# A layer-norm root begun on GpSimd, and sums and copies placed elsewhere in their queues

## The chip, the core and the metric

The kernel runs on one core of a Trainium2 chip. The metric is the device time of one execution, in microseconds. The core has TensorE (matrix products; PE, and PEld for its weight loads), VectorE (DVE), ScalarE (ACT), GpSimd (POOL) and SyncE (SP, which here issues the DMAs). Each engine works through its own queue in order; an instruction that waits holds up everything behind it on its engine.

## What is computed

Attention in blocks of 64 tokens, then two feed-forward layers over 4608 tokens of width 512. The reference, cut to what matters:

```python
scores = q_c @ k_c.T / sqrt(64); attn = softmax(scores); x = attn @ v_c      # chunks of 64
# first layer, 512 -> 2048 -> 512
h = x @ w_in;  g = h * clip(h + 3, 0, 6) / 6;  x = g @ w_out
# second layer, 512 -> 1024 -> 512
h = x @ w_in2
sm = exp(h - max(h)) / (sum(exp(h - max(h))) + 1e-9)
solu = h * sm
mu = mean(solu);  var = mean((solu - mu) ** 2)
out = ((solu - mu) / sqrt(var + 1e-6) * g_ln) @ w_out2
```

## The kernel before, in words

All products run in fp32 split into two parts (`hi`, a rounded copy made by ScalarE, and `lo`, the rest, made by a subtraction on VectorE or GpSimd), each product as three: hi by hi, hi by lo, lo by hi.

The first layer goes over 9 blocks of 512 tokens and, in each, over 16 slices `f` of the hidden width. For each slice `moe_h` makes h (L376), `moe_gate` the gate on VectorE (L386), `moe_split` the hi cast on ScalarE (L393) and the lo subtraction on VectorE (L396), and `moe_o` adds to the block's sum (L407). The attention of the next block is put between the slices.

The second layer works on pairs `p` of 128-token tiles (18 pairs, tiles 2p and 2p+1). Its first product is a two-by-two block product by Strassen's scheme: seven products `product_1` to `product_7` of six matmuls each (L560) in three PSUM banks a, b and c. `fetch_x2` (L520, SP) loads a pair's x, `combine_x2` (L525 to L528, four VectorE instructions) makes the sums and differences S1 to S4, `split_x2` makes hi on ScalarE (L534, L535) and lo on GpSimd (L541). The results are gathered while the banks go on being used: `product_1` is followed by a copy of bank a on ScalarE (L583), which `product_2` must wait for because it goes on adding to a; `sum_2` reads bank b on VectorE (L592), and `product_7` must wait for it; `sums_7` reads b and c (L611, L612), and `product_4` must wait for L611.

Then for each tile: `soft_1` (maximum L627 on VectorE, exponential with its sum L630 on ScalarE), `soft_2` (L635 to L642 on VectorE, of which L638 is the product of two SBUF operands over 128x1024), `turn` (a 32 by 32 transpose L648 on VectorE, and then copies of 32 partitions each (L666) by DMAs on SP, by ScalarE and for some tiles by GpSimd), `chain_square` (sum of squares, ScalarE, L673), `split_l` (hi on ScalarE, lo on GpSimd, L734 and L738), `out_mm` (24 matmuls, L754, called in turn by `out_next`), `out_store` (scaling by the root, ScalarE, L763, and the DMA out), called by `stores`. `chain_rstd` makes the inverse root of the variance of a pair of tiles: a shift of the bit pattern, a seed constant less that, and three Newton steps. Before, its first three instructions (L679, L684, L687, 128x2 each) are on VectorE, the twelve of the Newton steps (L692 to L697) on GpSimd.

The order on every engine is the order in which the code is written: it is a hand-made sequence. In slices 11 to 15 of the last block the products of pair 0 are mixed in; pairs 1, 2 and 3 have sequences of their own behind that, and pairs 4 to 17 run the `for p in range(3, NP)` loop. The prediction calls three stretches stage 1 (slice 15 and pair 1), stage 2 (the products of pair 3 up to `product_2(3)` and `product_7(3)`) and stage 3 (from tile 3's `out_mm` over `product_4(3)` to the products of pair 4).

Of the kernel before, what the change touches and what calls it, by code (L numbers as in the profile page):

```python
# [10 lines left out]
I32 = mybir.dt.int32  # L11
AF = mybir.ActivationFunctionType
ALU = mybir.AluOpType
# [8 lines left out]
def tile_kernel(  # L22
# [653 lines left out]

    def chain_rstd(p):
        va = va_t.pop(p)
        nc.vector.tensor_scalar(  # L679
            out=va, in0=va, scalar1=1.0 / FF2, scalar2=1e-6, op0=ALU.mult, op1=ALU.add  # L680
        )
        y = bs.tile([P, 2], F32, tag="y", name="y", bufs=4)
        yi = y.bitcast(I32)
        nc.vector.tensor_single_scalar(  # L684
            out=yi, in_=va.bitcast(I32), scalar=1, op=ALU.logical_shift_right
        )
        nc.vector.tensor_scalar(  # L687
            out=yi, in0=yi, scalar1=-1.0, scalar2=float(RSQRT_SEED), op0=ALU.mult, op1=ALU.add
        )
        tt = bs.tile([P, 2], F32, tag="tt", name="tt")  # L690
        for _ in range(3):
            nc.gpsimd.tensor_mul(out=tt, in0=y, in1=y)  # L692
            nc.gpsimd.tensor_mul(out=tt, in0=tt, in1=va)
            nc.gpsimd.tensor_scalar(
                out=tt, in0=tt, scalar1=-0.5, scalar2=1.5, op0=ALU.mult, op1=ALU.add
            )
            nc.gpsimd.tensor_mul(out=y, in0=y, in1=tt)  # L697
        for i in range(2):
            rs_t[2 * p + i] = y[:, i : i + 1]
# [147 lines left out]
    for b in range(NB):  # L847
# [3 lines left out]
        for f in range(NF):  # L851
# [9 lines left out]
            else:  # L861
                if last:
                    split_w(3 if f == 10 else 1, nc.vector)
                g = moe_split(t, nc.vector)
            pend.append((b, f, g))
            if f % 4 == 3:
                slot(b, f)
# [14 lines left out]
            if last:  # L882
# [16 lines left out]
                    fetch_x2(2)  # L899
                for step in EARLY.get(f, ()):  # L900
                    step(0)
                if f == 14:
                    combine_x2(1)
                elif f == 15:
                    combine_x2(2)
    while pend:
        moe_o(*pend.pop(0))
    put("2", NF - 1, late.pop(NF - 1))
# [5 lines left out]
    ps_2 = ctx.enter_context(tc.tile_pool(name="ps_2", bufs=2, space=PSUM, reuse_waits="tile"))  # L914

    product_1(1)
    split_x2(2)
    fetch_x2(3)
    soft_1(1)
    product_6(1)  # L920
    sum_2(1)
    soft_1(0)
    product_2(1)
    product_7(1)
# [31 lines left out]
    chain_rstd(0)  # L956
    out_next()
    soft_2(3)
    turn(3)
    fetch_x2(4)  # L960
    square(3)
    soft_1(5)
    soft_2(2)
    out_next()
    product_1(3)
    product_6(3)
    sum_2(3)
    turn(2)
# [13 lines left out]
    for p in range(3, NP):  # L982
        last = 2 * p - 2
        if p > 3:
            product_1(p)
            split_l(last - 2)
            stores()
            product_6(p)
            product_5(p)
            sum_2(p)  # L990
# [20 lines left out]
        chain_rstd(p - 1)  # L1011
        product_4(p)
        product_3(p)
        stores()
        out_next()
        soft_first(p)
    split_l(last)
# [79 lines left out]
```

## Time and profile before

| what | value |
|---|---|
| median of 3 runs | 1289.9 us (1288.97 to 1291.45) |
| the profiled execution, its own time | 1289.6 us |
| its span, first to last instruction | 1287.8 us |
| TensorE busy | 1247.7 us (97% of the span), 6260 matmuls |
| VectorE busy | 908.9 us (71%) |
| ScalarE busy | 597.4 us (46%) |
| GpSimd busy | 252.2 us (20%) |
| mean granted TensorE clock | 0.992 |

The rest, 1.8 us, lies around the span. The granted clock is given as a share of full speed: 1.00 is 2.4 GHz and 0.50 is 1.2 GHz. Read the waits of TensorE first, since it is the busiest engine, then the timelines of the other engines at the places where TensorE waits. Lines are those of the kernel before.

### The profile page before, as it was taken

To read this page: it belongs to the slowest core of one execution; us is meant where nothing else is said; L and a number is where in the kernel's file an instruction comes from. 1 tells how busy PE (TensorE), PEld (TensorE's weight loads), DVE (VectorE), ACT (ScalarE), POOL (GpSimd) and SP (SyncE) were. 2 spreads that over 40 slices of the span, in tenths; PEclk is the share of its full clock that TensorE was granted. 3 is DMA by queue.
4 is the path that set the end of the run, shared out by engine and by line. 5 is a ranking of instruction groups with operands and counts; after the bars stand their busy time and mean duration, and the time that the engine had idled before them with its cause. 6 is when DMAs were issued, how large, how long until landed. Compare 5 with 4: busy or idle time off the path is not lost.

```text
span 1287.8 us, 17624 instructions
## 1 busy us (share of the span) xinstructions
PE 1247.7 (97%) x6260; PEld 1024.5 (80%) x6260; DVE 908.9 (71%) x1720; ACT 597.4 (46%) x1097; POOL 252.2 (20%) x333
## 2 busy tenths in 40 slices
PE   5899999999999999999999999999869999999998
PEld 4688888888888888888888888887658888888887
DVE  6999556556556565565565565599888888888884
ACT  4776322222222222222322322463567777777775
POOL 1000000000000000000000000002456676666755
PEclk9999999999999999999999999999889999999999
DMA  9901101101101101101101100450112222323211
GB/s 320 374 26 47 61 25 44 64 25 48 59 25 49 58 25 50 58 25 50 58 25 50 58 25 1 147 180 17 58 50 81 90 89 77 95 70 95 91 56 64
DMA packets 68391, 93.70 MB, mean 73 GB/s; under 512 B 10192, under 2 KB 39120, under 8 KB 68304
## 3 DMA queue, kind: packets, MB, share of 16 engines
q1 hardware_dynamic: 68304, 92.58, 22.1%
q8 instruction: 49, 0.80, 0.3%
q14 instruction: 38, 0.31, 0.1%
HBM read 62.92 MB, written 18.87 MB: 64 GB/s over the span
## 4 chain that ended last, share of the span: by engine, by line
PE 86%; DVE 10%; ACT 2%; issue 1%; SPq 1%; DMA 1%; POOL 0%; DVEq 0%; ACTq 0%
PE acc L407 27%; PE hp L376 27%; PE po L754 14%; PE b L560 5%; PE c L560 4%; PE a L560 3%; PE att L355 3%; PE att L279 2%; DVE s L181 2%; DVE t L386 1%; ACT g_hi L393 1%; DVE s L173 1%; DVE g_lo L396 1%; DVE pbd L345 0%; DVE wo L181 0%
## 5 line engine op out<-in xcount | busy, mean ns | idle before, releaser
L407 PE MATMUL acc<-g_hi,wo 128*128 128x512 f32 x1152 | 289.3, 393 | 1.7 <-ACT g_hi L393 1.7
L376 PE MATMUL hp<-x_hi,wi 128*128 128x512 f32 x1152 | 285.7, 390 | 4.1 <-ACT wi L255 2.6
L382 ACT ACTIVATE t<-hp,three 128x512 f32<-128x512 f32 x144 | 99.1, 688 | 375.1 <-PE hp L376 374.6
L376 PEld LDWEIGHTS hp<-x_hi,wi 128*128 128x128 f32 x1152 | 215.6, 188 | 50.1 <-ACT wi L255 3.5
L407 PEld LDWEIGHTS acc<-g_hi,wo 128*128 128x128 f32 x1152 | 213.6, 188 | 51.3 <-issue 5.3
L386 DVE SCALAR_TENSOR_TENSOR t<-t,hp 128x512 f32<-128x512 f32 x144 | 98.9, 687 | 205.2 <-ACT t L382 205.1
L77 POOL TENSOR_TENSOR wi<-s,wi 128x512 fp32r<-128x512 f32 x5 | 7.3, 1453 | 875.4 <-ACT wi L76 869.1
L396 DVE TENSOR_TENSOR g_lo<-t,g_hi 128x512 fp32r<-128x512 f32 x144 | 99.6, 692 | 83.6 <-ACT g_hi L393 83.0
L407 PE MATMUL acc<-g_lo,wo 128*128 128x512 f32 x576 | 154.1, 389 | 0.0
L376 PE MATMUL hp<-x_lo,wi 128*128 128x512 f32 x576 | 153.9, 389 | 0.0
L754 PE MATMUL po<-wi,wo 128*128 128x512 f32 x648 | 150.8, 389 | 0.0
L393 ACT CAST g_hi<-t 128x512 fp32r<-128x512 f32 x144 | 89.3, 620 | 121.6 <-DVE t L386 121.6
L754 PEld LDWEIGHTS po<-wi,wo 128*128 128x128 f32 x648 | 121.5, 188 | 25.4 <-POOL wo L738 0.2
L345 DVE STREAM_TRANSPOSE pbd<-p 32x128 f32<-32x128 f32 x448 | 135.5, 303 | 5.7
L407 PEld LDWEIGHTS acc<-g_lo,wo 128*128 128x128 f32 x576 | 108.1, 188 | 22.8
L376 PEld LDWEIGHTS hp<-x_lo,wi 128*128 128x128 f32 x576 | 108.1, 188 | 22.5
L666 ACT COPY wo<-wo 32x256 f32<-32x256 f32 x228 | 92.0, 404 | 23.1 <-DVE wo L648 13.8
L541 POOL TENSOR_TENSOR x_lo<-xr,x_hi 128x768 fp32r<-128x768 f32 (+1 forms) x32 | 67.6, 2133 | 83.0 <-ACT x_hi L534 76.3
L638 DVE SCALAR_TENSOR_TENSOR wo<-wo,r,wo 128x1024 f32<-128x1024 f32 x36 | 77.0, 2139 | 1.3
L738 POOL TENSOR_TENSOR wo<-wo,wo 128x1024 fp32r<-128x1024 f32 x26 | 65.2, 2508 | 15.4 <-DMA xr<-x2d 7.3
L292 ACT ACTIVATE p<-p 128x512 f32<-128x512 f32 x29 | 18.3, 632 | 67.5 <-DVE p L289 67.5
L630 ACT ACTIVATE wo<-wo,nmx 128x1024 f32<-128x1024 f32 x36 | 41.5, 1153 | 13.8 <-DVE nmx L627 13.0
(205 smaller groups left out, 1599.6 us busy)
## 6 DMA issues: line engine op xcount, KB each, us to landing
wi<-in_moe_w_in SPq DMA_DIRECT2D x24, 512.0 KB, 7.5
wo<-wo SPq DMA_DIRECT2D x328, 32.0 KB, 1.9
wo<-in_moe_w_out SPq DMA_DIRECT2D x19, 512.0 KB, 8.3
x2d<-xo SPq DMA_DIRECT2D x36, 256.0 KB, 2.9
out<-ob SPq DMA_DIRECT2D x36, 256.0 KB, 2.2
v<-in_v SPq DMA_DIRECT2D x34, 256.0 KB, 2.6
xr<-x2d SPq DMA_DIRECT2D x34, 256.0 KB, 3.2
q<-in_q SPq DMA_DIRECT2D x33, 256.0 KB, 3.5
```

What stands on the lines that cost most here:

```text
L345: nc.vector.transpose(out=pb[o : o + 32, s // 2, c, s % 2], in_=pv[s * 32 : s * 32 + 32, c, e],)
L376: nc.tensor.matmul(hp, wi[f][:, a, kk * P : (kk + 1) * P], b[:, kk], start=(n == 0), stop=(n == 3 * KD - 1),)
L382: nc.scalar.activation(out=t, in_=hp, func=AF.Relu, bias=three[:])
L386: nc.vector.scalar_tensor_tensor(out=t, in0=t, scalar=6.0, in1=hp, op0=ALU.min, op1=ALU.mult)
L393: nc.scalar.copy(out=g_hi, in_=t)
L396: eng.tensor_sub(out=g_lo, in0=t, in1=g_hi.bitcast(F32))
L407: nc.tensor.matmul(acc[dc], wo[f][:, w, dc * P : (dc + 1) * P], g[i], start=(f == 0 and n == 0), stop=(f == NF - 1 and n == 2),)
L541: eng.tensor_sub(out=lo[:, f], in0=r, in1=hi[:, f].bitcast(F32))
L560: nc.tensor.matmul(ps, x[:, AT[a], j], w2[w, j][i], start=(start and n == 0), stop=(stop and n == 5), skip_group_check=True,)
L638: nc.vector.scalar_tensor_tensor(out=h, in0=e, scalar=r, in1=h, op0=ALU.mult, op1=ALU.mult, accum_out=mu)
L666: move(out=m[b * 32 : b * 32 + 32, a], in_=tr[a * 32 : a * 32 + 32, b])
L754: nc.tensor.matmul(po, a[f], wi[KD * NS + f][:, w], start=(n == 0), stop=(n == 3 * NF2 - 1),)
```

## The change

The root: `va` is scaled on GpSimd, and the shift and the subtraction from the seed, two instructions on VectorE, become one GpSimd instruction, a multiplication of the bit pattern (taken as an integer) by -0.5 and the addition of the seed. For each of the 18 pairs three VectorE instructions go and two GpSimd ones come. The rest are moves: `combine_x2(1)` stands behind slice 15's gate, between the cast and the subtraction of `moe_split`; `combine_x2(2)` behind pair 1's `sum_2`, with `split_x2(2)` and `fetch_x2(3)` behind it; `fetch_x2(4)` ahead of `turn(3)`'s copies; `product_1(3)`, which carries the copy of bank a, ahead of `soft_1(5)`; in the loop `stores()` ahead of `split_l`, and for p = 3 no `stores()` at all between `product_3` and `out_next`.

```diff
--- before.py
+++ after.py
@@ -676,16 +676,13 @@
 
     def chain_rstd(p):
         va = va_t.pop(p)
-        nc.vector.tensor_scalar(
+        nc.gpsimd.tensor_scalar(
             out=va, in0=va, scalar1=1.0 / FF2, scalar2=1e-6, op0=ALU.mult, op1=ALU.add
         )
         y = bs.tile([P, 2], F32, tag="y", name="y", bufs=4)
-        yi = y.bitcast(I32)
-        nc.vector.tensor_single_scalar(
-            out=yi, in_=va.bitcast(I32), scalar=1, op=ALU.logical_shift_right
-        )
-        nc.vector.tensor_scalar(
-            out=yi, in0=yi, scalar1=-1.0, scalar2=float(RSQRT_SEED), op0=ALU.mult, op1=ALU.add
+        nc.gpsimd.tensor_scalar(
+            out=y.bitcast(I32), in0=va.bitcast(I32), scalar1=-0.5, scalar2=float(RSQRT_SEED),
+            op0=ALU.mult, op1=ALU.add,
         )
         tt = bs.tile([P, 2], F32, tag="tt", name="tt")
         for _ in range(3):
@@ -861,7 +858,7 @@
             else:
                 if last:
                     split_w(3 if f == 10 else 1, nc.vector)
-                g = moe_split(t, nc.vector)
+                g = moe_split(t, nc.vector, (lambda: combine_x2(1)) if last and f == NF - 1 else None)
             pend.append((b, f, g))
             if f % 4 == 3:
                 slot(b, f)
@@ -899,10 +896,6 @@
                     fetch_x2(2)
                 for step in EARLY.get(f, ()):
                     step(0)
-                if f == 14:
-                    combine_x2(1)
-                elif f == 15:
-                    combine_x2(2)
     while pend:
         moe_o(*pend.pop(0))
     put("2", NF - 1, late.pop(NF - 1))
@@ -914,11 +907,12 @@
     ps_2 = ctx.enter_context(tc.tile_pool(name="ps_2", bufs=2, space=PSUM, reuse_waits="tile"))
 
     product_1(1)
-    split_x2(2)
-    fetch_x2(3)
     soft_1(1)
     product_6(1)
     sum_2(1)
+    combine_x2(2)
+    split_x2(2)
+    fetch_x2(3)
     soft_1(0)
     product_2(1)
     product_7(1)
@@ -956,13 +950,13 @@
     chain_rstd(0)
     out_next()
     soft_2(3)
+    fetch_x2(4)
     turn(3)
-    fetch_x2(4)
     square(3)
+    out_next()
+    product_1(3)
     soft_1(5)
     soft_2(2)
-    out_next()
-    product_1(3)
     product_6(3)
     sum_2(3)
     turn(2)
@@ -983,8 +977,8 @@
         last = 2 * p - 2
         if p > 3:
             product_1(p)
+            stores()
             split_l(last - 2)
-            stores()
             product_6(p)
             product_5(p)
             sum_2(p)
@@ -1011,7 +1005,8 @@
         chain_rstd(p - 1)
         product_4(p)
         product_3(p)
-        stores()
+        if p > 3:
+            stores()
         out_next()
         soft_first(p)
     split_l(last)
```

TensorE's order of instructions is unchanged. VectorE in slice 15 of the last block; L386 is the gate, L525 to L528 the combine of pair 1, L396 the lo half of the gate's result:

```order
 L617 TENSOR_TENSOR wo_7201<-s_7072,att 128x512
+L386 SCALAR_TENSOR_TENSOR t<-t,hp 128x512
 L525 TENSOR_TENSOR wo_6851<-wo_6850 128x256
 L526 TENSOR_TENSOR wo_6851<-wo_6850 128x256
 L527 TENSOR_TENSOR wo_6851<-wo_6851,wo_6850 128x256
 L528 TENSOR_TENSOR wo_6851<-wo_6850,wo_6851 128x256
-L386 SCALAR_TENSOR_TENSOR t<-t,hp 128x512
 L396 TENSOR_TENSOR g_lo<-t,g_hi 128x512
```

The gate has moved in front of the four instructions of the combine.

VectorE in stage 1, before; L525 to L528 are the combine of pair 2, L420 the first layer's last sums, L592 the sum of bank b of pair 1, L611 the sum of b behind `product_7`:

```order
L525 TENSOR_TENSOR xr_6855<-xr_6854 128x256
L526 TENSOR_TENSOR xr_6855<-xr_6854 128x256
L527 TENSOR_TENSOR xr_6855<-xr_6855,xr_6854 128x256
L528 TENSOR_TENSOR xr_6855<-xr_6854,xr_6855 128x256
L420 TENSOR_SCALAR xo<-acc_6555 128x512
L420 TENSOR_SCALAR xo<-acc_6557 128x512
L627 TENSOR_REDUCE nmx<-wo_7201 128x1
L592 TENSOR_TENSOR u_7378<-s_7354,b 128x512
L627 TENSOR_REDUCE nmx<-wo_7138 128x1
L611 TENSOR_TENSOR u_7406<-s_7354,b 128x512
```

and the same stretch now:

```order
L420 TENSOR_SCALAR xo<-acc_6555 128x512
L420 TENSOR_SCALAR xo<-acc_6557 128x512
L627 TENSOR_REDUCE nmx<-wo_7201 128x1
L592 TENSOR_TENSOR u_7364<-s_7350,b 128x512
L525 TENSOR_TENSOR xr_6855<-xr_6854 128x256
L526 TENSOR_TENSOR xr_6855<-xr_6854 128x256
L527 TENSOR_TENSOR xr_6855<-xr_6855,xr_6854 128x256
L528 TENSOR_TENSOR xr_6855<-xr_6854,xr_6855 128x256
L627 TENSOR_REDUCE nmx<-wo_7138 128x1
L611 TENSOR_TENSOR u_7406<-s_7350,b 128x512
```

The combine of pair 2 has moved from ahead of the sum L592 to behind it, and stands now ahead of the second maximum and of L611.

VectorE at the root of pair 0, before; L635 to L642 belong to `soft_2(3)`:

```order
L627 TENSOR_REDUCE nmx<-wo_7391 128x1
L679 TENSOR_SCALAR va<-va 128x2
L684 TENSOR_SCALAR y<-va 128x2
L687 TENSOR_SCALAR y<-y 128x2
L635 TENSOR_SCALAR r<-r 128x1
L636 RECIPROCAL r<-r 128x1
L638 SCALAR_TENSOR_TENSOR wo_7408,mu<-wo_7528,r,wo_7408 128x1024
```

Now L635 follows L627 at once there, and GpSimd has, with the line numbers of the changed kernel (L679 and L683 begin the root; L541 is the lo half of pair 3's x):

```order
L541 TENSOR_TENSOR x_lo<-xr_7376,x_hi 128x768
L541 TENSOR_TENSOR x_lo<-xr_7377,x_hi 128x1024
L679 TENSOR_SCALAR va<-va 128x2
L683 TENSOR_SCALAR y<-va 128x2
L689 TENSOR_TENSOR tt<-y 128x2
L690 TENSOR_TENSOR tt<-tt,va 128x2
```

The root's first instructions have moved from VectorE's queue into GpSimd's, behind the same subtractions.

ScalarE in stage 2, before; L666 are copies of tile 3, L583 the copy of bank a of pair 3, L630 behind it or ahead of it the exponential of tile 5:

```order
L673 ACTIVATE wo_7628,va<-wo_7408 128x1024
L666 COPY wo_7614<-wo_7612 32x256 x8
L630 ACTIVATE wo_7640,r<-wo_7497,nmx 128x1024
L583 COPY s_7681<-a 128x512
L673 ACTIVATE wo_7703,va<-wo_7391 128x1024
L734 CAST wo_7705<-wo_7614 128x1024
```

and now:

```order
L673 ACTIVATE wo_7627,va<-wo_7408 128x1024
L666 COPY wo_7617<-wo_7615 32x256 x8
L583 COPY s_7669<-a 128x512
L630 ACTIVATE wo_7673,r<-wo_7497,nmx 128x1024
L673 ACTIVATE wo_7702,va<-wo_7391 128x1024
L731 CAST wo_7704<-wo_7617 128x1024
```

The copy of bank a has moved ahead of the exponential.

## Rows read from the trace of the kernel before

**Rows 1.** Busy time by stretch: stretch, length, busy us (instructions) per engine, granted clock, DMA.

```profile
980.00:1240.00 260.00, 260.00 (x1149) 215.29 (x1148) 223.98 (x361) 200.42 (x368) 169.59 (x209) 1.00 0.28 86
951.30:978.00 26.70, 20.73 (x76) 16.43 (x76) 22.97 (x35) 20.68 (x40) 15.92 (x19) 0.83 0.23 70
910.72:917.47 6.75, 6.75 (x19) 5.32 (x19) 2.92 (x6) 2.40 (x5) 0.54 (x1) 0.60 0.42 110
949.59:954.34 4.75, 4.75 (x13) 3.75 (x13) 3.52 (x3) 3.99 (x8) 1.90 (x1) 0.57 0.49 141
965.90:970.99 5.09, 5.08 (x12) 3.99 (x13) 4.78 (x12) 4.32 (x11) 4.19 (x13) 0.52 0.17 46
20.00:30.00 10.00, 6.38 (x69) 5.06 (x66) 7.45 (x15) 5.19 (x10) 0.00 (x0) 1.00 1.04 380
```

**Rows 2.** Waits of TensorE in 780 to 1290 us: us in total, times, longest.

```profile
PE b L560 <- DVE u L611: 6.0, 1, 6.0
PE a L560 <- ACT s L583: 5.8, 1, 5.8
PE b L560 <- DVE u L592: 5.0, 1, 5.0
PE acc L407 <- ACT g_hi L393: 1.1, 1, 1.1
```

**Rows 3.** Timeline of VectorE, 895 to 911 us: start, length, engine, line, operation.

```profile
895.75 0.42 DVE L525 TENSOR_TENSOR wo<-wo 128x256 f32<-128x256 f32 x1
...
897.22 0.68 DVE L386 SCALAR_TENSOR_TENSOR t<-t,hp 128x512 f32<-128x512 f32 x1
...
902.01 0.93 DVE L525 TENSOR_TENSOR xr<-xr 128x256 f32<-128x256 f32 x1
...
907.67 1.27 DVE L420 TENSOR_SCALAR xo<-acc 128x512 f32<-128x512 f32 x2
...
908.87 1.20 DVE L627 TENSOR_REDUCE nmx<-wo 128x1 f32<-128x1024 f32 x1
...
910.00 0.67 DVE L592 TENSOR_TENSOR u<-s,b 128x512 f32<-128x512 f32 x1
```

**Rows 4.** Timeline of VectorE, 935 to 944 us.

```profile
935.13 1.24 DVE L679 TENSOR_SCALAR va<-va 128x2 f32<-128x2 f32 x1
...
940.43 0.14 DVE L635 TENSOR_SCALAR r<-r 128x1 f32<-128x1 f32 x1
...
943.17 1.25 DVE L648 STREAM_TRANSPOSE wo<-wo 128x1024 f32<-128x1024 f32 x1
```

**Rows 5.** Timeline of ScalarE, 947 to 953 us; idle time ahead in brackets.

```profile
947.82 1.15 ACT L630 ACTIVATE wo<-wo,nmx 128x1024 f32<-128x1024 f32 x1
...
948.97 0.56 ACT L583 COPY s<-a 128x512 f32<-128x512 f32 x1
...
951.32 1.05 ACT L734 CAST wo<-wo 128x1024 fp32r<-128x1024 f32 x1 [0.73 <-DMA wo<-wo]
```

**Rows 6.** Timeline of GpSimd, 936 to 941 us.

```profile
936.31 4.18 POOL L541 TENSOR_TENSOR x_lo<-xr,x_hi 128x768 fp32r<-128x768 f32 x2
```

**Rows 7.** Three lines' own views, 900 to 1288 us: ns min/median/max.

```profile
L638 DVE SCALAR_TENSOR_TENSOR wo<-wo,r,wo x36: 1283/2232/3460, 917.2 to 1264.2; 128x1024 f32<-128x1024 f32 x36
...
L687 DVE TENSOR_SCALAR y<-y x18: 168/169/2319, 938.2 to 1277.6; 128x2 int32<-128x2 int32 x18
...
L694 POOL TENSOR_SCALAR tt<-tt x54: 191/191/1135, 942.2 to 1280.7; 128x2 f32<-128x2 f32 x54
```

**Rows 8.** Timeline of VectorE, 952 to 966 us.

```profile
952.64 2.46 DVE L525 TENSOR_TENSOR xr<-xr 128x256 f32<-128x256 f32 x1 [1.23 <-DMA xr<-x2d]
...
959.85 0.17 DVE L679 TENSOR_SCALAR va<-va 128x2 f32<-128x2 f32 x1
...
964.04 1.23 DVE L648 STREAM_TRANSPOSE wo<-wo 128x1024 f32<-128x1024 f32 x1
```

**Rows 9.** Timeline of TensorE in the attention's start, 22 to 24 us.

```profile
22.76 0.63 PE L330 MATMUL att<-ident,wo 128*128 128x128 f32 x4 [2.44 <-DVE wo L322]
```

## The prediction

> **What bounds the kernel now.** Read the busy time by stretch first. From 980 to 1240 us TensorE is busy for 260.00 of 260 us at a granted clock of 1.00 (2.4 GHz), while VectorE, ScalarE and GpSimd have 36, 60 and 90 us to spare [rows 1]. In the loop nothing but TensorE sets the time, so a faster root there is worth nothing. The price of one matmul is read from the same row: 260 / 1149 = 0.226 us, so six cost 1.36 us and the 24 of an `out_mm` 5.43 us.
>
> Next read TensorE's waits behind 780 us. There are four: 1.1 us ahead of slice 15's sum, 5.0 us for L592, 5.8 us for L583 and 6.0 us for L611 [rows 2], 17.9 us in all. Behind each of the three long ones the granted clock is down, 0.60, 0.57 and 0.52 on the mean over the stretches that follow, where 0.50 is 1.2 GHz [rows 1]. Of the matmuls listed there 18, 12 and 12 lie wholly inside; at 0.226 us they would take 4.07, 2.72 and 2.72 us, and they took 6.75, 4.75 and 5.09. The lower clock costs 2.7 + 2.0 + 2.4 = 7.1 us. So the change has 17.9 + 7.1 = 25.0 us to win, all of it ahead of 980 us, and each wait has its own cause in VectorE's and ScalarE's queues.
>
> A wait of about 2 us need not bring the clock down: in the attention's start TensorE waits 2.44 us once [rows 9] and the granted clock of that stretch is 1.00 [rows 1]. Between that and 5.0 us the trace shows nothing.
>
> **Part 1, stage 1: the combines of pairs 1 and 2.** The gate of slice 15 began at 897.22 because the combine of pair 1 took the time from 895.75, 1.47 us [rows 3]. It now begins 1.47 us earlier, and the cast behind it too. TensorE waited 1.13 us for that cast. I take that wait to be gone: 1.1 us. The subtraction of the gate's lo half comes behind the combine now, but no later than before, since it waited for the cast anyway.
>
> The combine of pair 2 began at 902.01 and the next instruction at 907.67: 5.66 us on VectorE for four instructions that took 1.47 us for pair 1 [rows 3]. The sum L592, at 910.00, stood behind it. Moved in front, L592 starts 5.66 us earlier, and some 0.7 us more since the subtractions ahead of it begin earlier: at 903.6, done at 904.3. TensorE, 1.1 us earlier itself, ends `product_2(1)` at about 904.4, and `product_7(1)` need not wait. The 5.0 us and the 2.7 us of clock behind them are gone.
>
> What is late next is L611, which `product_4(1)` needs. TensorE has two products (2.7 us) until then, to about 907.1. VectorE has the combine of pair 2, a maximum of 1.13 us (908.87 to 910.00) and L611 itself, of L592's kind at 0.67 us [rows 3]: 904.3 + 1.8 = 906.1 plus the combine. The combine costs between 1.47 us (alone) and 5.66 us (between GpSimd's instructions). GpSimd still has the last weight's lo half and pair 2's first subtraction to do in that stretch, so I take the middle, 3.5 us: a wait of 2.5 us remains (0.4 to 4.6). **Stage 1: 1.1 + 5.0 + 2.7 - 2.5 = 6.3 us gained.**
>
> **Part 2, stage 2: the root of pair 0 and the copy of bank a.** On VectorE L679, L684 and L687 last from 935.13 to 940.43, 5.3 us [rows 4], for three instructions of which L687 has a median of 0.169 us and a longest of 2.319 us [rows 7]. While they ran GpSimd worked on two subtractions from 936.31 on for 4.18 us, to 940.49 [rows 6]; the three end as these end. They wait for GpSimd, rather than work. In the changed kernel L635 and L636 follow, and then L638, a product of two SBUF operands. L638 has a shortest time of 1.283 us and a median of 2.232 us [rows 7], so it is held up in the same way. I take it that L638 and L642 inherit half of the 5.3 us: `turn(3)` comes 2.7 us earlier (5.3 at best).
>
> The Trainium skill, "SBUF — State Buffer", section "Who interferes with whom", says that VectorE and GpSimd share a port pair which one instruction holds for its whole length, that `tensor_scalar` can need it and that an instruction with two SBUF inputs contends for it. By that rule the wait is handed on to L638, and stage 2 gives the 4.7 us worked out below; if the small instructions alone were slow, `turn(3)` would be 5.3 us earlier, only some 0.5 us of stage 2's waits would stay, it would give 7.3 us and the sum would be 1270.8 us. The longest and shortest times of L638 above agree with the rule.
>
> ScalarE's copy L583 also stood behind an exponential that held ScalarE from 947.82 to 948.97 [rows 5], and moves ahead of it: 1.2 us. So L583 comes 2.7 + 1.2 = 3.9 us earlier and 5.8 - 3.9 = 1.9 us of wait remain, below the 2.44 us which kept the clock: the 2.0 us of clock come back.
>
> Next, `out_mm(3)` needs the copies of `turn(3)`. Their cast L734 started at 951.32 [rows 5], 6.9 us after L648 ended (943.17 + 1.25 [rows 4]): eight DMAs one after another on SP. The fetch of pair 4 now stands ahead of these DMAs, but its tile comes free at about the time at which `turn(3)` ends, so I cost this at nothing; were the fetch late, its two issues would come on top, at most two eighths of those 6.9 us: 1.7 us. With `turn(3)` 2.7 us earlier L734 ends at 949.6. TensorE, which started `product_2(3)` at 949.59 and now does so 3.9 us earlier, is through with twelve matmuls at 948.4: 1.2 us of wait. **Stage 2: 5.8 + 2.0 - 1.9 - 1.2 = 4.7 us.**
>
> **Part 3, stage 3: the root of pair 1 and the fetch of pair 4.** L611 was late by 6.0 us. Ahead of it on VectorE the root of pair 1 lasted from 959.85 to 964.04, 4.2 us, and the combine of pair 4 waited 1.23 us for its fetch and then took 2.46 us for its first instruction [rows 8]. With the 2.7 us of stage 2 L611 comes 6.9 us earlier, and 8 to 10 with the fetch ahead of the eight DMAs; L638 of `soft_2(5)` may take part of it back. TensorE gets there 4.7 us earlier. So 6.0 - 9.0 + 4.7 = 1.7 us remain (0.7 to 3.8), and the 2.4 us of clock come back.
>
> Then ScalarE: between its cast L734 of tile 3 and its next copy of bank a it works 20.68 us [rows 1], of which one L763 has moved behind the copy (0.7 us): 20.0 us. It starts at 948.6, so that copy ends at about 969.2 at the earliest. TensorE from 949.6 on needs 5.43 + 1.7 + 2.72 + 5.43 + 4.07 = 19.3 us, to 968.9. ScalarE has waits of its own in there (6 us of 26.7 before), of which some stay; I take 1.5 us of wait at `product_2(4)` (0.3 to 3). **Stage 3: 6.0 + 2.4 - 1.7 - 1.5 = 5.2 us.**
>
> **Part 4: the loop and the rest.** GpSimd gets two small instructions for each pair. The nearest of its rows, L694, takes 0.191 us, at most 1.135 [rows 7]; the 128x2 integer form is not in the trace. A pair lasts 90 matmuls or 20.4 us and GpSimd works 169.59 / 260 x 20.4 = 13.3 us of it [rows 1], so 0.4 us more (up to 2.3) hide in 7.1 us of idle time. VectorE is relieved of 14 roots there and `stores()` changes place; TensorE has no wait in the loop that they could shorten. Both cost nothing.
>
> **The sum.** 6.3 + 4.7 + 5.2 = 16.2 us off the profiled execution's 1289.6 us is 1273.4 us. The median of the runs is 0.3 us above that execution, which I leave out.
>
> **The rivals.**
> A. The remaining waits are shorter: the combine of pair 2 meets an idle GpSimd (0.4 instead of 2.5), L638 inherits nothing, L583 and L611 are on time. For it speaks that GpSimd's work also shifts. Of the 25.0 us about 21 are then won: 1268.6 us.
> B. The clock stays low. Each of the places keeps a wait of 1.2 to 2.5 us, several close together, and the trace clears only 2.44 us as a single wait. Then the 7.1 us of clock do not come back: 1280.5 us.
> C. The change does not do what it says in stages 2 and 3: L638 and L642 inherit all of the roots' time, because GpSimd's subtractions have to be done in any case, and the waits move to them. Stage 1 and the 1.2 us of L583's move remain, 7.5 us: 1282.1 us. Against it: L638 alone would have to last 6 us, and its row has 3.46 us as the longest.
> D. Slower: GpSimd's integer instruction is costly. Above 7.1 us for the two of a pair GpSimd cannot follow and sets the pace of the loop's 14 pairs; 16.2 us of gain are used up at 1.2 us more, 8.3 us for the two. At 9 us: 1.9 x 14 = 27 us later, 1300 us. Against it: it has the same shape and two operations as L694, at 0.2 us.
> E. No change: the queues regain the old order of waits at another place, ScalarE above all, which has no slack for 20 us in stage 3. About 1289 us.
>
> **Chances.** Forecast 0.45, A 0.23, B 0.20, C 0.06, D 0.03, E 0.03. A measurement of this kernel can tell 0.2% (2.6 us) from no change. Faster by more: forecast, A, B and C, 0.94; within: 0.03; slower: 0.03. The range takes in the forecast with the bounds of its terms, most of A and B: 1266 to 1281 us.
>
> **What would show it.** Right: TensorE's waits behind 890 us are each below 3 us and sum to some 9 us in place of 17.9; the granted clock stays at or near 1.00 in the three stretches; L679's group is on GpSimd at about 0.2 us each; L638 of `soft_2(3)` and `soft_2(5)` is well above 1.3 us; the loop's stretch is full as before. Wrong: a stretch at 0.50 (B); a wait for GpSimd's L541, L738 or y in the loop (D); L583 or L611 still the cause of 5 us (C); no wait over 1 us left (A).

## The result and the profile after

The changed kernel takes 1274.2 us (median of 4 runs, 1272.99 to 1275.23) against 1290.4 us in the same comparison; the ratio is 0.9875 with a 95% interval of 0.9858 to 0.9892. That is 16.2 us faster, where 16.2 us were forecast (from 1289.6 to 1273.4 us). The profiled execution took 1273.3 us, its span 1271.6 us, with a mean granted clock of 0.998.

The timeline of TensorE in the changed kernel, its rows that waited (start, length, line, operation; in brackets the wait and what ended it), the answer to [rows 2]. Lines behind the root are three lower now: L735 was L738, L751 was L754, L760 was L763:

```profile
907.80 0.73 PE L560 MATMUL b<-v,x_hi 128*128 128x512 f32 x2 [0.24 <-DVE u L611]
...
915.38 0.73 PE L560 MATMUL b<-pbd,x_hi 128*128 128x512 f32 x2 [0.46 <-DVE r L635]
...
937.80 1.21 PE L560 MATMUL a<-wi,x_hi 128*128 128x512 f32 x4 [0.96 <-ACT s L583]
...
941.88 5.73 PE L751 MATMUL po<-wi,wo 128*128 128x512 f32 x24 [1.02 <-ACT ob L760]
...
955.08 2.46 PE L751 MATMUL po<-wi,g_lo 128*128 128x512 f32 x8 [0.75 <-POOL g_lo L735]
...
961.82 1.20 PE L560 MATMUL a<-wi,x_hi 128*128 128x512 f32 x4 [0.18 <-ACT s L583]
...
965.49 0.73 PE L560 MATMUL b<-pbd,x_hi 128*128 128x512 f32 x2 [2.01 <-DVE u L592]
```

Seven waits of 5.6 us together stand where four of 17.9 us stood, and none is above 2.1 us. The busy time by stretch, behind the longest of them and in the loop (columns as in [rows 1]):

```profile
965.40:970.40 5.00, 4.91 (x21) 4.05 (x22) 4.83 (x11) 4.92 (x11) 4.04 (x11) 1.00 0.70 230
970.00:1230.00 260.00, 260.00 (x1149) 215.29 (x1148) 210.59 (x318) 198.79 (x364) 177.91 (x236) 1.00 0.27 84
```

The granted clock is 1.00 behind that wait, as in all the stretches where it had been 0.52 to 0.60. The loop is full as before: 260.00 of 260 us. VectorE is busy 13 us less in it (210.59 against 223.98) and GpSimd 8 us more (177.91 against 169.59), and neither matters.

Where the time came from, read from the start times of the same instructions in the two timelines of TensorE:

| up to | before | after | change | gained since the row above |
|---|---|---|---|---|
| slice 15, the products of pair 0 | 895.95 | 896.39 | +0.44 | |
| stage 1: `product_4(1)` | 916.01 | 907.80 | -8.21 | 8.65 |
| pair 2, up to `product_1(3)` | 939.59 | 932.32 | -7.27 | -0.94 |
| stage 2: `out_mm(3)` | 954.34 | 941.88 | -12.46 | 5.19 |
| stage 3: `out_mm(5)` | 983.27 | 966.98 | -16.29 | 3.83 |
| the span's end | 1287.8 | 1271.6 | -16.2 | 0 |

The 0.44 us of the first row stand already 15 us earlier (880.99 and 881.43), ahead of everything that was changed: the profiled executions of the kernels below pass that place between 880.99 and 883.44, so it is scatter and not an effect. Kernels are therefore compared further down by the distance from `product_4(1)`, the end of stage 1.

**Stage 1.** VectorE in the changed kernel, the answer to [rows 3]: the sum L592, the first and the last instruction of pair 2's combine, and L611:

```profile
903.77 0.68 DVE L592 TENSOR_TENSOR u<-s,b 128x512 f32<-128x512 f32 x1
904.37 0.52 DVE L525 TENSOR_TENSOR xr<-xr 128x256 f32<-128x256 f32 x1
...
905.60 0.43 DVE L528 TENSOR_TENSOR xr<-xr,xr 128x256 f32<-128x256 f32 x1
...
907.07 0.68 DVE L611 TENSOR_TENSOR u<-s,b 128x512 f32<-128x512 f32 x1
```

and GpSimd beside it:

```profile
902.05 2.56 POOL L77 TENSOR_TENSOR wi<-wo,wi 128x512 fp32r<-128x512 f32 x2
906.00 4.21 POOL L541 TENSOR_TENSOR x_lo<-xr,x_hi 128x768 fp32r<-128x768 f32 x2 [1.39 <-ACT x_hi L534]
```

L592 starts at 903.77 (forecast 903.6), and `product_7(1)` starts at 904.55 without a listed wait. The combine takes from 904.37 to 905.94, 1.57 us in place of 5.66. It falls into the hole between GpSimd's last weight subtraction, which ends at 904.6, and pair 2's first, which starts at 906.00.

**Stage 2.** L638, L642 and the transpose L648 of tile 3 on VectorE, to be read beside [rows 4 and 7]:

```profile
928.24 1.91 DVE L638 SCALAR_TENSOR_TENSOR wo<-wo,r,wo 128x1024 f32<-128x1024 f32 x1
...
930.38 2.02 DVE L642 TENSOR_SCALAR wo<-wo,mu 128x1024 f32<-128x1024 f32 x1
932.50 1.25 DVE L648 STREAM_TRANSPOSE wo<-wo 128x1024 f32<-128x1024 f32 x1
```

and GpSimd there:

```profile
926.65 2.42 POOL L735 TENSOR_TENSOR wo<-wo,wo 128x1024 fp32r<-128x1024 f32 x1 [1.77 <-ACT wo L731]
929.01 5.66 POOL L541 TENSOR_TENSOR x_lo<-xr,x_hi 128x768 fp32r<-128x768 f32 x2
934.76 0.19 POOL L679 TENSOR_SCALAR va<-va 128x2 f32<-128x2 f32 x1
935.03 0.19 POOL L683 TENSOR_SCALAR y<-va 128x2 int32<-128x2 int32 x1
```

L638 takes 1.91 and L642 2.02 us, where 1.28 and 0.75 us are their shortest. The integer instruction of the root (L683) takes 0.19 us on GpSimd.

ScalarE, beside [rows 5]: the copy of bank a, the cast of tile 3 and the stores of tiles 1 and 0:

```profile
937.16 0.59 ACT L583 COPY s<-a 128x512 f32<-128x512 f32 x1
...
940.19 1.05 ACT L731 CAST wo<-wo 128x1024 fp32r<-128x1024 f32 x1
941.14 1.26 ACT L760 ACTIVATE ob<-po,y 128x512 f32<-128x512 f32 x2
```

`out_mm(3)` started at 941.88, not when the cast ended (941.24) but when the first of the two stores, done at about 941.8, had read the bank that it writes.

**Stage 3.** VectorE, beside [rows 8]: L611 of pair 3 in the kernel before (first row) and in the changed one, then L635 and L638 of tile 7 there:

```profile
965.21 0.64 DVE L611 TENSOR_TENSOR u<-s,b 128x512 f32<-128x512 f32 x1
...
946.98 0.65 DVE L611 TENSOR_TENSOR u<-s,b 128x512 f32<-128x512 f32 x1
...
960.20 0.15 DVE L635 TENSOR_SCALAR r<-r 128x1 f32<-128x1 f32 x1 [1.62 <-ACT wo L630]
...
960.59 3.26 DVE L638 SCALAR_TENSOR_TENSOR wo<-wo,r,wo 128x1024 f32<-128x1024 f32 x1
```

L611 starts at 946.98, before TensorE is through with `out_mm(3)`. What is late now is L592 of pair 4: L635 waited 1.62 us for ScalarE's exponential, and L638 then took 3.26 us.

### The profile page after: what moved, and what is told of

It is laid out like the page before. It is cut to its first block, busy times and chain, and to the rows that moved or that the text cites. A ratio compares the mean times of both kernels' runs of the same rounds, so it can differ in the third digit from the quotient of the medians.

```text
span 1271.6 us, 17613 instructions
## 1 busy us (share of the span) xinstructions
PE 1244.4 (98%) x6260; PEld 1020.5 (80%) x6260; DVE 883.5 (69%) x1666; ACT 596.8 (47%) x1097; POOL 262.5 (21%) x369
## 4 chain that ended last, share of the span: by engine, by line
PE 85%; DVE 9%; ACT 2%; issue 2%; POOL 1%; SPq 1%; DMA 1%; DVEq 0%; POOLq 0%; ACTq 0%
PE acc L407 28%; PE hp L376 28%; PE po L751 14%; PE b L560 4%; PE c L560 3%; PE att L355 3%; PE a L560 3%; PE att L279 2%; DVE s L181 2%; DVE t L386 1%; DVE g_lo L396 1%; ACT g_hi L393 1%; DVE s L173 1%; DVE wo L638 0%; SPq L666 0%
## 5 line engine op out<-in xcount | busy, mean ns | idle before, releaser
L386 DVE SCALAR_TENSOR_TENSOR t<-t,hp 128x512 f32<-128x512 f32 x144 | 98.9, 687 | 205.3 <-ACT t L382 205.0
L396 DVE TENSOR_TENSOR g_lo<-t,g_hi 128x512 fp32r<-128x512 f32 x144 | 99.6, 692 | 82.9 <-ACT g_hi L393 82.3
L751 PE MATMUL po<-wi,wo 128*128 128x512 f32 x648 | 151.0, 389 | 1.0 <-ACT ob L760 1.0
L751 PEld LDWEIGHTS po<-wi,wo 128*128 128x128 f32 x648 | 121.5, 188 | 26.8 <-ACT ob L760 1.4
L666 ACT COPY wo<-wo 32x256 f32<-32x256 f32 x228 | 92.0, 404 | 16.8 <-DVE wo L648 10.2
L541 POOL TENSOR_TENSOR x_lo<-xr,x_hi 128x768 fp32r<-128x768 f32 (+1 forms) x32 | 70.0, 2208 | 70.5 <-ACT x_hi L534 70.5
L638 DVE SCALAR_TENSOR_TENSOR wo<-wo,r,wo 128x1024 f32<-128x1024 f32 x36 | 75.3, 2092 | 1.3
L735 POOL TENSOR_TENSOR wo<-wo,wo 128x1024 fp32r<-128x1024 f32 x26 | 65.0, 2499 | 6.8 <-issue 2.5
L630 ACT ACTIVATE wo<-wo,nmx 128x1024 f32<-128x1024 f32 x36 | 41.5, 1153 | 18.1 <-DVE nmx L627 17.9
```

The lines of the kernel that those rows point to most:

```text
L386: nc.vector.scalar_tensor_tensor(out=t, in0=t, scalar=6.0, in1=hp, op0=ALU.min, op1=ALU.mult)
L396: eng.tensor_sub(out=g_lo, in0=t, in1=g_hi.bitcast(F32))
L541: eng.tensor_sub(out=lo[:, f], in0=r, in1=hi[:, f].bitcast(F32))
L638: nc.vector.scalar_tensor_tensor(out=h, in0=e, scalar=r, in1=h, op0=ALU.mult, op1=ALU.mult, accum_out=mu)
L666: move(out=m[b * 32 : b * 32 + 32, a], in_=tr[a * 32 : a * 32 + 32, b])
L751: nc.tensor.matmul(po, a[f], wi[KD * NS + f][:, w], start=(n == 0), stop=(n == 3 * NF2 - 1),)
```

## The experiments

Gains are against the kernel before in the same comparison (1290.1 to 1290.6 us). The intervals of the ratios are near 0.0015 to either side, 2 us, so smaller differences between two variants are read from the waits and not from the time.

| kernel | median us | gain us | ratio (95% interval) |
|---|---|---|---|
| the change | 1274.2 | 16.2 | 0.9875 (0.9858 to 0.9892) |
| root alone | 1283.0 | 7.3 | 0.9943 (0.9926 to 0.9959) |
| combines alone | 1282.65 | 7.6 | 0.9937 (0.9922 to 0.9952) |
| combines and fetch | 1277.4 | 12.7 | 0.9899 (0.9885 to 0.9914) |
| combines and root | 1275.2 | 14.9 | 0.9882 (0.9867 to 0.9897) |
| the change, root back | 1276.7 | 13.5 | 0.9891 (0.9877 to 0.9906) |
| the change, pair 2's combine back | 1281.1 | 9.2 | 0.9926 (0.9911 to 0.9941) |
| the change, fetch back | 1275.65 | 15.0 | 0.9886 (0.9869 to 0.9902) |
| the change, copy back | 1273.9 | 16.8 | 0.9872 (0.9857 to 0.9887) |
| the change, stores back | 1274.3 | 15.7 | 0.9873 (0.9857 to 0.9890) |
| the change, tile 7's exponential first | 1273.1 | 17.0 | 0.9864 (0.9849 to 0.9878) |

### The combines

Pairs 1 and 2 moved, nothing else:

```diff
-                g = moe_split(t, nc.vector)
+                g = moe_split(t, nc.vector, (lambda: combine_x2(1)) if last and f == NF - 1 else None)
...
-                if f == 14:
-                    combine_x2(1)
-                elif f == 15:
-                    combine_x2(2)
...
     sum_2(1)
+    combine_x2(2)
+    split_x2(2)
+    fetch_x2(3)
```

> The kernel before with only the combines of pairs 1 and 2 moved (and the split and fetch that stand behind the second). Theory: the waits of 1.1 and 5.0 us go, the clock stays at 1.00 in stage 1, and the waits of stages 2 and 3 are as before (5.8 and 6.0 us): 7.5 to 8.5 us faster, about 1282 us. Rival (a gain in stage 1 is given back at the next wait, since VectorE and ScalarE set stage 2 and do not move up): the waits of stage 2 grow by what stage 1 wins, time within 2 us of before.

It gained 7.6 us. TensorE's two long waits there:

```profile
942.07 2.07 PE L560 MATMUL a<-wi,x_hi 128*128 128x512 f32 x4 [5.76 <-ACT s L583]
...
958.38 1.22 PE L560 MATMUL b<-v,x_hi 128*128 128x512 f32 x2 [5.44 <-DVE u L611]
```

The long waits of stage 1 are gone and those of stages 2 and 3 stay at 5.8 and 5.4 us: what stage 1 wins is not given back there.

The other way round, the change with pair 2's combine, split and fetch back:

```diff
+                if f == 15:
+                    combine_x2(2)
...
     product_1(1)
+    split_x2(2)
+    fetch_x2(3)
...
     sum_2(1)
-    combine_x2(2)
-    split_x2(2)
-    fetch_x2(3)
```

> The changed kernel with the combine, split and fetch of pairs 2 and 3 back at their old places; the combine of pair 1 stays moved. Theory: the wait for L592 of pair 1 comes back at about 5 us with the clock at 0.50 behind it, 7 us slower than the changed kernel (1281 us), and the wait of 1.1 us in slice 15 stays away, so the combine of pair 1 is worth 1.1 us and that of pair 2 the other 7 to 7.5. Rival (the order of GpSimd's and VectorE's instructions in stage 1 matters more than the sum's place): the wait for L592 comes back at below 3 us and the clock holds, 2 to 4 us slower.

It gained 9.2 us, 7.0 less than the change. The longest wait is that for L592 of pair 1 again, and the one of slice 15 stays away:

```profile
911.70 1.22 PE L560 MATMUL b<-pbd,x_hi 128*128 128x512 f32 x2 [5.39 <-DVE u L592]
```

The granted clock of the 5 us behind it is 0.50, as expected. So pair 2's combine is worth some 7 us; pair 1's about 1 us is read from its wait, since the times (7.6 and 7.0 us) can't tell it from nothing.

### The root

```diff
-        nc.vector.tensor_scalar(
+        nc.gpsimd.tensor_scalar(
             out=va, in0=va, scalar1=1.0 / FF2, scalar2=1e-6, op0=ALU.mult, op1=ALU.add
...
-        nc.vector.tensor_single_scalar(
-            out=yi, in_=va.bitcast(I32), scalar=1, op=ALU.logical_shift_right
-        )
-        nc.vector.tensor_scalar(
-            out=yi, in0=yi, scalar1=-1.0, scalar2=float(RSQRT_SEED), op0=ALU.mult, op1=ALU.add
+        nc.gpsimd.tensor_scalar(
+            out=y.bitcast(I32), in0=va.bitcast(I32), scalar1=-0.5, scalar2=float(RSQRT_SEED),
+            op0=ALU.mult, op1=ALU.add,
```

> The kernel before with the root alone begun on GpSimd (two instructions there for three on VectorE), nothing moved. Theory (half of the root's time on VectorE is handed on to the next instructions, the rest is won): stage 1 as before (waits 1.1 and 5.0 us, low clock behind), the wait for L583 falls from 5.8 to 2.4 us, that for L611 from 6.0 to about 3 us, and the clock behind the first of the two comes back: 7 to 9 us faster than before, about 1282 us. Rival 1 (all of it is handed on, since GpSimd's subtractions must be done anyway): both waits stay within 1 us of 5.8 and 6.0, time within 1.5 us of before. Rival 2 (none is handed on): the wait for L583 below 1 us, that for L611 about 1 us, 13 us or more faster.

It gained 7.3 us, and the waits of stages 2 and 3 fell to 2.1 and 2.2 us, as the theory of a part handed on has it; both rivals are out. The clock was expected to come back behind the first of them and did not (0.66 in the next 5 us, last section):

```profile
946.43 1.43 PE L560 MATMUL a<-wi,x_hi 128*128 128x512 f32 x4 [2.08 <-ACT s L583]
...
958.68 0.73 PE L560 MATMUL b<-v,x_hi 128*128 128x512 f32 x2 [2.18 <-DVE u L611]
```

The change with the root back on VectorE (the same lines the other way round):

> The changed kernel with the root's first three instructions back on VectorE, all moves kept. Theory (stage 1 does not need the root): the 8 us of stage 1 stay; the wait for L583 is 1.0 + 3.4 = about 4.4 us, so the clock falls behind it; the wait for L611 comes back to some 2 to 4 us: 6 to 9 us slower than the changed kernel, 1280 to 1283 us. Rival (the moves are what wins, the root adds nothing): within 2 us of the changed kernel. If the parts add up, the gain of the root alone and this loss are the same number within 2 us.

This lost only 2.7 us, less than half of what was expected (its four runs, 1276.5 to 1277.1 us, lie above all of the change's). The wait for L583 came back as expected, but that for L611 did not:

```profile
942.01 2.08 PE L560 MATMUL a<-wi,x_hi 128*128 128x512 f32 x4 [4.62 <-ACT s L583]
...
952.91 0.73 PE L560 MATMUL b<-v,x_hi 128*128 128x512 f32 x2 [0.42 <-DVE u L611]
```

The root itself shows why; the first two rows are the first and the last instruction of pair 0's, the next two those of pair 1's, and the last two GpSimd's instructions on either side of pair 1's root:

```profile
928.67 1.24 DVE L679 TENSOR_SCALAR va<-va 128x2 f32<-128x2 f32 x1
...
931.75 2.31 DVE L687 TENSOR_SCALAR y<-y 128x2 int32<-128x2 int32 x1
...
949.92 0.16 DVE L679 TENSOR_SCALAR va<-va 128x2 f32<-128x2 f32 x1
...
950.31 0.17 DVE L687 TENSOR_SCALAR y<-y 128x2 int32<-128x2 int32 x1
...
945.54 2.40 POOL L738 TENSOR_TENSOR wo<-wo,wo 128x1024 fp32r<-128x1024 f32 x1 [6.65 <-DMA wo<-wo]
952.37 5.18 POOL L541 TENSOR_TENSOR x_lo<-xr,x_hi 128x768 fp32r<-128x768 f32 x2 [4.43 <-ACT x_hi L534]
```

For pair 0 it takes 5.3 us as before, for pair 1 from 949.92 to 950.48, 0.6 us in place of 4.2. The instructions are the same. With the early fetch the combine and the split of pair 4 run at other times, and at the root of pair 1 GpSimd is not in a subtraction: it is idle from 947.9 to 952.4. In the kernel before it worked on pair 4's subtractions from 959.99 to 964.11, and that root lasted from 959.85 to 964.04. The price of the root on VectorE is the price of what GpSimd does at that moment.

That was tested directly. In the kernel before and in the changed one the two subtractions of pair 3 on GpSimd were replaced by copies on ScalarE:

```diff
+            if p == 3:
+                nc.scalar.copy(out=lo[:, f], in_=r)
+                return
             eng.tensor_sub(out=lo[:, f], in0=r, in1=hi[:, f].bitcast(F32))
```

> The kernel before, where the lo halves of pair 3's x are plain copies on ScalarE, which is idle there, in place of GpSimd's two subtractions (so pair 3's lo halves hold wrong values). Theory (the root's three small instructions wait for GpSimd's): L679, L684 and L687 of pair 0 together take 0.5 to 2 us in place of 5.3, the rest being GpSimd's subtraction of tile 0, which stays. Rival (they are slow of themselves there, or wait for ScalarE): still over 4 us.

VectorE in this kernel (L682, L687 and L690 are the root's three instructions):

```profile
935.03 1.23 DVE L682 TENSOR_SCALAR va<-va 128x2 f32<-128x2 f32 x1
936.30 0.17 DVE L687 TENSOR_SCALAR y<-va 128x2 int32<-128x2 int32 x1
936.50 0.17 DVE L690 TENSOR_SCALAR y<-y 128x2 int32<-128x2 int32 x1
```

1.55 us until the next instruction in place of 5.3, of which 1.23 is the first one's wait, until GpSimd's subtraction of tile 0 ends. So the small instructions do wait for GpSimd. This single run took 1285.6 us.

> The changed kernel with the same replacement (pair 3's lo halves hold wrong values). Theory (L638 and L642 of tile 3 inherit the wait for GpSimd's subtractions): L638 falls from 1.9 to 1.3 us and L642 from 2.0 to 0.75 us, and the wait for L583 of pair 3, 1.0 us, goes. Rival (they are long for another reason): both stay within 0.3 us.

L638 and L642 have the lines L641 and L645 here:

```profile
928.08 1.91 DVE L641 SCALAR_TENSOR_TENSOR wo<-wo,r,wo 128x1024 f32<-128x1024 f32 x1
...
930.23 0.76 DVE L645 TENSOR_SCALAR wo<-wo,mu 128x1024 f32<-128x1024 f32 x1
```

L642 fell from 2.02 to 0.76 us, as expected. L638 stayed at 1.91: half a miss. It starts at 928.08, while GpSimd's subtraction of tile 0 runs until about 929, so its wait is for that one and not for pair 3's. The wait for L583 is gone, but this single run took 1273.6 us: the 1.4 us that it was ahead of the changed kernel at `product_7(4)` (964.13 against 965.49) are gone at `product_7(5)` (986.28 against 986.04), behind a stretch of lower clock (last section).

### The fetch, and how it stands to the root

> The changed kernel with the fetch of pair 4 back behind the copies of tile 3. Theory (the fetch's place is worth more than the root's second pair: it lets the combine of pair 4 run without a wait and keeps GpSimd's subtraction of pair 4 away from what follows): VectorE waits 3 to 4 us ahead of the combine of pair 4, L611 is late by about 3 us at product_4(3), the time is 3 to 5 us above the changed kernel (1277 to 1279 us). Rival (ScalarE's queue in stage 3 sets the time in any case): the wait at L611 takes the place of the waits behind it, within 1.5 us of the changed kernel.

```diff
     soft_2(3)
-    fetch_x2(4)
     turn(3)
+    fetch_x2(4)
```

In the changed kernel this lost 1.2 us, less than expected and too little to be told by the time. The first instruction of pair 4's combine waited for the fetch and was long, and TensorE waited for L611:

```profile
943.05 2.54 DVE L525 TENSOR_TENSOR xr<-xr 128x256 f32<-128x256 f32 x1 [2.26 <-DMA xr<-x2d]
```

```profile
952.32 1.04 PE L560 MATMUL b<-v,x_hi 128*128 128x512 f32 x2 [3.08 <-DVE u L611]
```

Here a wait of 3.1 us stands at L611 and none comes behind it; in the changed kernel L611 was on time and waits of 0.75, 0.18 and 2.01 us, 2.9 in all, came behind it. The waits nearly cancel, so the rival was right in what takes whose place. What is left of the loss is of the size of a fall of the clock (last section), and the granted clock behind the 3.1 us is 0.66.

The fetch beside the combines, without the root (the diffs of the combines, and the one above reversed):

> The kernel before with the combines of pairs 1 and 2 moved and the fetch of pair 4 ahead of tile 3's copies; root, copy and stores as before. Theory (the early fetch alone removes the wait for L611: the combine runs at once, and the root of pair 1 no longer meets GpSimd's subtraction of pair 4): the wait for L583 stays 5.8 us, that for L611 falls from 5.4 to about 1 us, 4 to 6 us faster than with the combines alone (1282.7): about 1277.5 us. Rival (the fetch is only worth what it was beside the root, 1.5 us): 1281 us, the wait for L611 at 4 us.

It gained 5.0 us over the combines alone, as expected. The wait for L583 is untouched, that for L611 falls from 5.4 to 2.05 us (1 was expected):

```profile
942.46 2.08 PE L560 MATMUL a<-wi,x_hi 128*128 128x512 f32 x4 [5.71 <-ACT s L583]
...
955.31 0.72 PE L560 MATMUL b<-v,x_hi 128*128 128x512 f32 x2 [2.05 <-DVE u L611]
```

And the root beside the combines, without the fetch (the diffs of the combines and of the root):

> The kernel before with the combines of pairs 1 and 2 moved and the root on GpSimd; fetch, copy and stores as before. Theory (fetch and root stand in for each other: with either one stage 3 falls back to what VectorE's and ScalarE's queues allow): the wait for L583 about 2.1 us and for L611 about 2.2 us, as with the root alone; 7 us faster than with the combines alone, 1275 to 1276 us. Rival (the parts do not add to the combines): 1279 us or more.

It gained 7.3 us over the combines alone, as much as the root gains by itself, so combines and root add up: 14.9 of the change's 16.2 us. What the fetch, the copy and the stores add to these two, 1.3 us, is within the scatter. The wait for L583 is 2.10 us as expected, that for L611 3.06 (2.2 expected). So beside the combines the fetch is worth 5.0 us and the root 7.3, but behind the fetch and the rest the root adds 2.7, and behind the root and the rest the fetch adds 1.2. They stand in for each other: both bring L611 and the combine of pair 4 forward, and the time then hangs on something that neither moves (next section).

### The copy and the stores

> The changed kernel with pair 3's copy of bank a (L583) back behind the exponential of tile 5. Theory (what ends last behind it is the store of tile 1, which frees the bank of out_mm(3), and that store stands behind copy and exponential alike): the wait for L583 grows from 1.0 to 2.3 us, the wait of 1.0 us ahead of out_mm(3) goes, and the time is within 0.8 us of the changed kernel (1274 to 1275 us). Rival (the place of the copy is worth the exponential's 1.3 us, as the prediction counted it): 1.3 us slower or more.

```diff
-    out_next()
-    product_1(3)
     soft_1(5)
     soft_2(2)
+    out_next()
+    product_1(3)
```

The time did not change (1273.9 us). The wait for L583 grew to 2.1 us and the one ahead of `out_mm(3)` is gone:

```profile
939.42 1.25 PE L560 MATMUL a<-wi,x_hi 128*128 128x512 f32 x4 [2.10 <-ACT s L583]
...
943.87 5.61 PE L751 MATMUL po<-wi,wo 128*128 128x512 f32 x24
...
966.01 0.73 PE L560 MATMUL b<-pbd,x_hi 128*128 128x512 f32 x2 [1.76 <-DVE u L592]
```

The theory had the time right and the reason wrong. The granted clock behind the 2.1 us is 0.66, and `out_mm(3)` starts 35.6 us behind `product_4(1)` (908.30 here) where it is 34.1 in the changed kernel: it is 1.5 us late, and the store of tile 1 does not hold it. Yet `product_7(4)`, the last row, starts 57.7 us behind `product_4(1)` in both (965.49 less 907.80 there), because the waits of 0.75 us at tile 2's `out_mm` and of 0.18 us at `product_2(4)` are not there and that for L592 of pair 4 is shorter. By the traces L592 hangs on GpSimd, whose last subtraction ahead of it, tile 5's, is this one in the changed kernel:

```profile
960.38 2.39 POOL L735 TENSOR_TENSOR wo<-wo,wo 128x1024 fp32r<-128x1024 f32 x1 [0.22 <-PE b L560]
```

L592 starts 1.98 us behind its end (962.77 and 964.75). In all ten kernels in which this order stands and L592 waits for nothing else (all but the kernel before, that kernel with pair 3's subtractions replaced, the combines alone, and the one of the next section) it is 1.98 or 1.99 us, although L638 in between lasts from 1.41 to 3.27 us. GpSimd works from its subtraction of pair 4 at 948.14 up to there without a pause above 0.3 us, the root of pair 1 included. That stretch begins 40.3 us behind `product_4(1)` with the copy at either place, so the copy did not change what comes at its end.

> The changed kernel with the stores at their old places in the loop (behind split_l, and for p = 3 a store between product_3 and out_next). Theory (ScalarE is what product_2(4) and product_7(4) wait for, and the store of tile 3 stands ahead of tile 7's exponential again): the wait for L592 of pair 4 grows from 2.0 by 0.6 us or L583's by as much, within 1 us of the changed kernel. Rival (the order of the stores in all the loop matters): over 2 us slower, with new waits of TensorE behind 980 us.

```diff
             product_1(p)
-            stores()
             split_l(last - 2)
+            stores()
...
-        if p > 3:
-            stores()
+        stores()
```

The stores at their old places gave 1274.3 us, no difference that can be told. GpSimd's stretch begins 40.4 us behind `product_4(1)` here, and `product_7(4)` again starts 57.7 us behind it. The wait did not grow but moved from L592 (0.16 us left) to the copy L583, behind the store on ScalarE; the granted clock of the next 5 us is 0.66:

```profile
964.23 1.20 PE L560 MATMUL a<-wi,x_hi 128*128 128x512 f32 x4 [2.02 <-ACT s L583]
```

### Tile 7's exponential first

The wait of 2.0 us for L592 of pair 4 is the longest left, so for p = 3 the cast of tile 5, and GpSimd's work on it, was put behind tile 7's exponential:

```diff
-        split_l(last + 1)
-        chain_rstd(p - 1)
+        if p > 3:
+            split_l(last + 1)
+            chain_rstd(p - 1)
...
-        soft_first(p)
+        if p > 3:
+            soft_first(p)
+        else:
+            soft_1(2 * p + 1)
+            split_l(last + 1)
+            soft_1(2 * p)
+            soft_2(2 * p + 1)
+            chain_rstd(p - 1)
```

> The changed kernel, for p = 3 alone with the exponential of tile 7 (L630) ahead of the split of tile 5 (the cast on ScalarE, the subtraction and the root on GpSimd). Theory (the wait of 2.0 us for L592 of pair 4 comes from L638 of tile 7, which starts late behind the cast and then meets GpSimd's subtraction): L638 of tile 7 starts 0.9 us earlier and takes 1.3 in place of 3.3 us, the wait for L592 goes: 1.5 to 2.5 us faster than the changed kernel, 1272 to 1273 us. Rival (the late cast of tile 5 holds up its out_mm or GpSimd, and what is won returns as a wait there): within 0.7 us of the changed kernel.

L638 of tile 7 fell from 3.26 to 1.31 us as expected, but L642 behind it now took the wait, 2.72 in place of 0.75 us, while GpSimd's subtraction of tile 5 ran from 962.18 to 964.56:

```profile
960.86 1.31 DVE L638 SCALAR_TENSOR_TENSOR wo<-wo,r,wo 128x1024 f32<-128x1024 f32 x1
...
962.40 2.72 DVE L642 TENSOR_SCALAR wo<-wo,mu 128x1024 f32<-128x1024 f32 x1
```

The wait for L592 fell to 1.06 us and not to none. This is the only run that moves that subtraction, and it moves ScalarE's work too, so that L592 hangs on it is read from the traces and not shown by a change of that alone. 1273.1 us is the lowest median of all these kernels, 1.1 us below the change; the intervals overlap, so it is not shown to be faster.

## Why the prediction was right, point by point

**Stage 1, forecast 6.3 us, measured 8.65.** The wait of slice 15 and that for L592 went, the clock came back, and L611 was next, all as written. Mis-sized was the combine of pair 2: 3.5 us taken as the middle of 1.47 and 5.66, 1.57 us measured, since GpSimd was between two subtractions. The wait that was to be 2.5 us is 0.24. The combines alone and the combine put back (7.6 and 7.0 us) agree with a stage worth about 8 less what pair 2 gives back.

**Pair 2, forecast nothing, measured -0.94.** The prediction left out that stage 1's new order puts `soft_2(1)`'s L638 beside pair 2's subtractions (2.46 us in the changed kernel). Small waits of TensorE follow, 0.46 us the longest listed.

**Stage 2, forecast 4.7, measured 5.2.** That half of the root's 5.3 us is handed on: `turn(3)` moved up by 10.67 us (943.17 to 932.50), 7.27 of them before stage 2, so by 3.4 where 2.7 were taken. The handing on is shown by the replaced subtractions, in L642 above all. The Trainium skill, "SBUF — State Buffer", section "Who interferes with whom", calls it an exclusive lock on a shared port pair, and these runs agree: 5.3 us became 1.55 us when two GpSimd instructions were taken away. The copy's 1.2 us count within stage 2, where `out_mm(3)` starts 1.5 us later without the move, but they are given back at `product_7(4)`, which the prediction did not see. The wait ahead of `out_mm(3)`, 1.0 us against 1.2 forecast, is for the store of tile 1 and not for the cast and the DMAs ahead of it: that its size was met is luck.

**Stage 3, forecast 5.2, measured 3.8.** The wait for L611 went wholly, where 1.7 us were to remain. From tile 3's transpose L648 to L611 VectorE takes 22.0 us before (943.17 to 965.21) and 14.5 in the changed kernel (932.50 to 946.98), 18.0 with the fetch put back and 15.5 with the root put back. So the root is worth 4.1 us there, as the prediction had it (4.2), and the fetch behind it 3.5, where 1.1 to 3.1 were taken: L611 came 11.0 us earlier and not 9.0. Costed the other way round the fetch is worth 6.5 us and the root behind it 1.0; the two overlap by 3 us, and only their order in the sum kept that from being counted twice. Too small was the floor behind L611. The prediction put it on ScalarE and took 1.5 us of wait at `product_2(4)`. By TensorE's start times 0.4 us were lost there, 1.4 at tile 2's `out_mm` (6.84 us to the next product in place of 5.48), for GpSimd's lo halves, and 2.3 at `product_7(4)` (3.67 us behind `product_2(4)` in place of 1.36), behind GpSimd's subtraction of tile 5. That is 4.1 us against the 3.2 that were to remain in all, and GpSimd's queue, on which by the traces the largest part hangs, is not in the prediction's stage 3.

**The loop**, forecast at nothing: 260.00 of 260 us in both. L683's 0.19 us rules out rival D. Rival C, that all is handed on, falls with the root alone (7.3 us gained; L638 and L642 of tile 3 take over 1.9 of the 5.3 us), and rival E with the time. Rival B, the lower clock, did not come in the profiled execution, though it could have (last section). Of rival A's 21 us only stage 1's part came.

The total agrees better than its terms: +2.3 (stage 1), -0.9 (pair 2), +0.5 and -1.4, and 0.4 us of scatter ahead of slice 15. The causes were mostly foreseen; that their sum is met within 0.1 us is luck.

## What to carry to other kernels

When a small VectorE instruction takes 2 us, look first at what GpSimd runs there: here it was waiting for GpSimd's subtractions, and when it was moved away the next VectorE instructions took over part of the wait. Two edits that each cure the same wait are not to be added; cost the second with the first already made. And when a queue is relieved, ask on which engine the next release hangs: here a copy moved forward gained 1.5 us at the next `out_mm` and nothing at the end, where by the traces GpSimd's queue set the time.

## What the runs showed of the hardware that was not expected

The prediction took a wait of about 2 us as harmless to TensorE's clock, from one wait of 2.44 us [rows 9]. The runs do not bear that out. Ten waits of 1.99 to 2.18 us stand in the profiles of these kernels. Behind five of them the granted clock of the next 5 us was 0.66, so part of it at 1.2 GHz (root alone 2.08, copy back 2.10, stores back 2.02, and 1.99 and 2.01 in the two kernels with pair 3's subtractions replaced), and behind five 1.00 (the change 2.01, root alone 2.18, pair 2's combine back 1.99, combines and fetch 2.05, combines and root 2.10). The kernel with the root alone has both, behind 2.08 and behind 2.18 us (columns as in [rows 1]):

```profile
946.40:951.40 5.00, 4.97 (x15) 3.94 (x16) 3.87 (x3) 4.24 (x8) 2.89 (x5) 0.66 0.46 135
958.60:963.60 5.00, 4.92 (x21) 4.05 (x22) 4.83 (x8) 4.31 (x11) 5.00 (x4) 1.00 0.16 43
```

15 matmuls against 21 in the same 5 us: the fall costs, by estimate, about 1.4 us (6 x 0.226). The two waits of 3.1 us (the fetch put back; combines and root) were followed by 0.66 and 0.70. What decides it the runs do not show; it is not the length of the wait or its place alone, since a wait of 2.10 us ahead of `product_2(3)` was followed by 0.66 with the copy back and by 1.00 with combines and root. It would explain why what was gained with pair 3's subtractions replaced did not show in the time: there the wait of 2.01 us for L592 of pair 4 was followed by 0.66, in the changed kernel the same 2.01 us by 1.00.
